# Loading the first filter block in two transfers, warming TensorE on a ready constant, and a new instruction order

## The chip, the cores and the metric

The kernel runs on one core of one Trainium2 chip. The metric is the device time of one execution in microseconds (us), the median of several. Before the change it is 344.8 us (three runs, 344.19 to 345.65).

The engines are named as in the profile: PE is TensorE (PEld its weight loads), DVE is VectorE, ACT is ScalarE, POOL is GpSimd, SP is SyncE, which issues most DMAs.

## What is computed

Two layers, each a long convolution block (A) and a gated feed-forward block (B), on 2048 positions of 512 channels in bf16. `q` is the stream x; the other inputs are k, v, a 4-tap filter, a 2048-tap filter per channel, a diagonal, and three weight matrices.

```python
def A(xn, k, v, shift_k, ssm_k, ssm_D):
    kv = causal_fir4(k, shift_k) * v
    y = causal_conv(kv, ssm_k)          # 2048 taps per channel, by FFT in the reference
    return xn * (y + kv * ssm_D)

def B(xn, w_gate, w_up, w_down):        # 512 -> 1792 -> 512
    return (silu(xn @ w_gate) * (xn @ w_up)) @ w_down

x = q
for layer in (0, 1):                    # same k, v and weights in both layers
    x = x + A(layernorm(x), k, v, shift_k, ssm_k, ssm_D)
    x = x + B(layernorm(x), w_gate, w_up, w_down)
```

## The kernel before, in words

**Tiling.** The 2048 positions are cut into four blocks c = 0 to 3 of 512; each block is 128 partitions of four consecutive rows (r = 0 to 3). A feed-forward unit is (layer, c, half): two of the four row sets, 256 columns on PE. There are 16 units, each with 224 matmuls of 256 columns (`pf`, gate and up, L311 through the helper `mm`) and 28 of 512 columns (`pd`, down, L990).

**The convolution** is done block by block with discrete Fourier transforms written as matmuls: `hn` (filter, channels on partitions) is transposed by PE into `pt`, copied to `hs`, transformed with the table `fwd` into `ps`, evacuated to `ev` and folded to `G`. The k block `kn` is transposed into `kTb` (L366, copies at L372 and L374), the 4-tap filter is 64 matmuls of `kTb` against diagonal tables `dg` (L311, `ps<-dg,kTb`), their result is multiplied by v (`vt`, L524, DVE), and `vt` is transformed (L458) into `X`. Products `X*G` give `Z`, `m`; inverse transforms (L797) give y for block 0. Then LayerNorm, product with y, the second LayerNorm, `z`, its transpose `zT`, and the first feed-forward matmul. The work up to there is called the opening here. The convolutions of the later blocks are threaded between the feed-forward matmuls.

**The opening's loads.** SP issues, in this order: `hn` of block 0 (L342, one transfer of 512 KB, 1 KB pieces), `kn` (L352), `vt`, `xc` (q), `hn` and `vt` of block 1, `wg_sb`, then DMA transposes and the other weights. Each is 512 KB but for the weights. ACT issues the two small ones, `tapR` and `drow` (L1067, L1069). DMAs share eight completion semaphores in turn, so the ninth waits for the first, and so on.

**Warming matmuls.** `warm` (L1264) issues matmuls that nobody reads, wherever the plan has PE idle in the first 32 us. Their operands are `wz`, a tile that DVE sets to 0.5 (L1050).

**LayerNorm statistics.** Most come from DVE (`ln_stats`, L809 to L812). Eight of them come from ACT (`ln_stats_act`): sums with accumulators (L828, L834), then `ve = sum/D + eps` on ACT (L838), then `rstd = ve^-0.5` on POOL (L840).

**The order.** Every operation is recorded with an engine, a cost and its reads and writes (`Plan.add`). The list `ORDER` ranks all 1568 operations; `Plan.order` sorts by it and gives each tile a slot of its ring, `Plan.issue` emits the sorted list. Each engine runs its instructions in that order. PSUM rings that matter in the opening: `pf` with four slots (transposes of `hn`, all `ps` of the first block, the `pf` tiles of the feed-forward), `pc` and `pd` with two each (transposes of `kn`, filter results).

What stands on PE at the start before: 22 warming matmuls, 4 small transposes of the taps (L1133), 5 warming, 16 transposes of `hn` (L477), 8 of `kn`, 8 transforms of `hs`, 8 transposes of `kn`, 6 transforms, 64 filter matmuls, 2 transforms, then the transforms of `vt`.

Of the kernel before, what the change touches and what calls it, by code (L numbers as in the profile page):

```python
# [9 lines left out]
P = 128  # L10
# [32 lines left out]
H_SPLIT = False  # L43
# [7 lines left out]
LASTV = True  # L51
ORDER = [
# [186 lines left out]
def kernel(  # L239
# [1024 lines left out]
    def warm(ring, slot, n):  # L1264
        t = psp.tile([P, P], F32, name="wm", tag=f"{ring}{slot}")
        for _ in range(n):
            nc.tensor.matmul(t[:], lhsT=wz.t[:], rhs=wz.t[:], start=True, stop=True)  # L1267
# [33 lines left out]
```

## Time and profile before

| what | value |
|---|---|
| median of three runs | 344.8 us |
| the profiled execution | 344.93 us |
| its span, first to last instruction | 343.2 us |
| PE busy | 336.4 us (98%), 2579 matmuls on record |
| DVE busy | 283.4 us (83%) |
| ACT busy | 253.9 us (74%) |
| POOL busy | 35.3 us (10%) |
| first feed-forward matmul starts | 33.58 us |
| last PE work ends | about 340.0 us |

The profiled execution is 1.73 us longer than its span; what lies outside the span is not seen. PE counts as busy while a matmul is in its pipe, so matmuls that follow each other closely overlap in the record; how far apart their starts are tells the rate, and the chain of waits, which sets such pieces end to end, shows it directly.

### The profile page before, as it was taken

Reading aid. Unit: us, or ns where it says so; the run is one execution under the profiler, and the core shown is the slowest. Engines: PE = TensorE matmul, PEld = TensorE weight load, DVE = VectorE, ACT = ScalarE, POOL = GpSimd, SP = SyncE. Lnnn points to the kernel's source line nnn. Section 1 sums busy time; section 2 is a strip of 40 time slices with the busy share of each in tenths; the row PEclk is TensorE's granted clock in tenths of the full one; section 3 lists DMA queues with packets and bytes.
Section 4 is the critical chain, followed back from the end, with each engine's and each line's share of the span. In section 5 each row is a group of like instructions: output and inputs, shape, how many; then the busy total and the mean of one; then the engine's idle time right before and its main releaser. Section 6 shows DMA issues by size and latency. Waiting matters only on the chain.

```text
span 343.2 us, 6553 instructions
## 1 busy us (share of the span) xinstructions
PE 336.4 (98%) x2579; PEld 248.6 (72%) x2610; DVE 283.4 (83%) x482; ACT 253.9 (74%) x504; POOL 35.3 (10%) x46
## 2 busy tenths in 40 slices
PE   8999999999999999999999999999999999999996
PEld 7756868768687676858586777768685877777783
DVE  8899999899999999899999999989998433726022
ACT  6999999899997765958789995779475464446261
POOL 4010100203111000103110100201101001000000
PEclk9999999999999999999999999999999999999999
DMA  7999218310116044040101014210101100110101
GB/s 273 336 316 341 52 27 112 77 32 0 34 31 94 14 95 138 2 94 3 32 2 46 2 46 79 76 32 1 32 0 33 35 13 0 39 39 8 24 26 37
DMA packets 42088, 22.95 MB, mean 67 GB/s; under 512 B 33861, under 2 KB 39882, under 8 KB 42058
## 3 DMA queue, kind: packets, MB, share of 16 engines
q1 hardware_dynamic: 41904, 22.47, 26.6%
q8 instruction: 20, 0.33, 0.4%
q14 instruction: 10, 0.08, 0.1%
q10 hardware_dynamic: 154, 0.07, 0.1%
HBM read 12.33 MB, written 2.10 MB: 42 GB/s over the span
## 4 chain that ended last, share of the span: by engine, by line
PE 91%; ACT 4%; DVE 3%; issue 1%
PE pf L311 54%; PE pd L990 28%; PE ps L311 6%; PE ps L458 1%; ACT H L419 1%; PE wm L1267 1%; DVE bnst L809 1%; ACT hs L487 1%; PE pt L477 1%; ACT X L419 0%; ACT n L859 0%; PE pt L366 0%; DVE m L540 0%; DVE t L665 0%; DVE Z L667 0%
## 5 line engine op out<-in xcount | busy, mean ns | idle before, releaser
L311 PE MATMUL pf<-zT,wu_sb 128*128 128x256 bf16 x896 | 110.4, 273 | 0.1
L311 PE MATMUL pf<-zT,wg_sb 128*128 128x256 bf16 x896 | 110.2, 273 | 0.2
L990 PE MATMUL pd<-wd_sb,ht 128*128 128x512 bf16 (+1 forms) x440 | 102.4, 372 | 1.2
L311 PEld LDWEIGHTS <-wu_sb 128*128 128x128 bf16 x896 | 87.7, 98 | 16.4
L311 PEld LDWEIGHTS <-wg_sb 128*128 128x128 bf16 x896 | 87.6, 98 | 16.5 <-issue 0.8
L974 ACT CAST ht<-pf 128x512 bf16<-128x512 f32 x112 | 64.0, 591 | 29.3 <-PE pf L311 29.1
L970 ACT ACTIVATE sg<-pf 128x512 bf16<-128x512 f32 x112 | 65.5, 603 | 17.4 <-PE pf L311 15.1
L990 PEld LDWEIGHTS <-ht 128*128 128x128 bf16 x462 | 45.2, 98 | 42.5
L977 DVE TENSOR_TENSOR ht<-ht,sg 128x1024 bf16<-128x1024 bf16 (+1 forms) x64 | 39.0, 617 | 24.0 <-ACT sg L970 18.7
L814 POOL TENSOR_TENSOR rstd<-ve,nhalf 128x2 f32<-128x2 f32 x24 | 23.0, 958 | 217.8 <-DVE ve L812 207.6
L1034 ACT CAST dn<-pd 128x512 bf16<-128x512 f32 x30 | 17.0, 589 | 21.0 <-PE pd L990 20.9
L809 DVE BATCH_NORM_STATS2 bnst<-xc 128x6 f32<-128x512 bf16 x48 | 31.6, 684 | 0.6
L419 ACT ACTIVATE X<-ps 128x512 bf16<-128x512 f32 x32 | 19.2, 611 | 4.0 <-PE ps L311 3.4
L653 DVE TENSOR_TENSOR t<-X,G 128x2048 bf16<-128x2048 bf16 x18 | 21.9, 1218 | 0.1
L657 DVE TENSOR_TENSOR t<-X,G 128x2048 bf16<-128x2048 bf16 x18 | 21.9, 1216 | 0.0
L1037 DVE TENSOR_TENSOR xc<-xc,dn 128x1024 bf16<-128x1024 bf16 x15 | 10.3, 689 | 13.4 <-ACT dn L1034 13.2
L665 DVE TENSOR_TENSOR t<-t,t 128x2048 bf16<-128x2048 bf16 x12 | 14.7, 1222 | 0.3
L667 DVE TENSOR_TENSOR Z<-Z,t 128x2048 bf16<-128x2048 bf16 x12 | 14.6, 1220 | 0.2
L840 POOL TENSOR_TENSOR rstd<-ve,nhalf 128x2 f32<-128x2 f32 x8 | 8.7, 1088 | 59.2 <-ACT ve L838 59.1
L419 ACT ACTIVATE H<-ps 128x512 bf16<-128x512 f32 x24 | 13.8, 610 | 0.1
L886 DVE TENSOR_TENSOR n<-n,Yk 128x1024 bf16<-128x1024 bf16 x15 | 10.3, 688 | 4.1 <-ACT n L859 3.8
L604 ACT ACTIVATE kc<-kTb,tapF 128x512 bf16<-128x512 bf16 x16 | 12.1, 783 | 0.0
(105 smaller groups left out, 323.3 us busy)
## 6 DMA issues: line engine op xcount, KB each, us to landing
hn<-in_A_ssm_k_dram SPq DMA_DIRECT2D x4, 512.0 KB, 4.1
vt<-in_A_v_dram SPq DMA_DIRECT2D x4, 512.0 KB, 5.9
xc<-in_A_q_dram SPq DMA_DIRECT2D x4, 512.0 KB, 5.3
out_dram<-xc SPq DMA_DIRECT2D x15, 128.0 KB, 1.8
wg_sb<-in_B_w_gate_dram SPq DMA_DIRECT2D x1, 1792.0 KB
wu_sb<-in_B_w_up_dram SPq DMA_DIRECT2D x1, 1792.0 KB, 8.5
wd_sb<-in_B_w_down_dram SPq DMA_DIRECT2D x1, 1280.0 KB, 12.0
kn<-in_A_k_dram SPq DMA_DIRECT2D x1, 512.0 KB, 4.5
```

Of the source, the lines that this page charges most:

```text
L311: nc.tensor.matmul(o, lhsT=lhsT, rhs=rhs, start=(n == 0), stop=(n == len(terms) - 1))
L419: add("ACT", act(D), lambda: nc.scalar.activation(out=view(), in_=ps.t[:], func=ACT.Copy, scale=scale), r=[ps], w=[(buf, keys)], conv=conv)
L653: dve(n * D, lambda t1=t1, part=part: nc.vector.tensor_mul(out=t1.t[:], in0=x.t[:, sl, 0, :], in1=g.t[:, sl, part, :]), [(x, key(slots, (0 ...
L657: dve(n * D, lambda t2=t2, part=part: nc.vector.tensor_mul(out=t2.t[:], in0=x.t[:, sl, 1, :], in1=g.t[:, sl, 1 - part, :]), [(x, key(slots ...
L665: dve(n * D, lambda t1=t1, t2=t2, comb=comb: nc.vector.tensor_tensor(out=t1.t[:], in0=t1.t[:], in1=t2.t[:], op=comb), [t2], [t1], conv=conv)
L809: add("DVE", 0.6, lambda st=st, i=i: nc.vector.bn_stats(out=st.t[:], in_=xs[c].t[:, i, :]), r=[(xs[c], (i,))], w=[st])
L814: add("POOL", pw, lambda: nc.gpsimd.tensor_tensor(out=rstd.t[:], in0=ve.t[:], in1=nhalf.t[:].to_broadcast((P, n)), op=ALU.pow), r=[ve, nha ...
L970: add("ACT", act(D), lambda ps=ps, o=o, sg=sg: nc.scalar.activation(out=sg.t[:, o:o + 2, :], in_=ps.t[:], func=ACT.Silu), r=[ps], w=[(sg, ...
L974: add("ACT", act(D), lambda ps=ps, o=o, ht=ht: nc.scalar.copy(out=ht.t[:, o:o + 2, :], in_=ps.t[:]), r=[ps], w=[(ht, (o // 2,))], due=(uni ...
L977: dve(n * W, lambda sg=sg, ht=ht: nc.vector.tensor_mul(out=ht.t[:], in0=ht.t[:], in1=sg.t[:]), [sg], [ht], due=(unit, k / pairs, 0.0, "h"))
L990: nc.tensor.matmul((pds[o] if not cs.start else pds[HP]).t[:, cs], lhsT=ht.t[:, q, o * P:(o + 1) * P], rhs=wt["d"].t[:, ft, cs], start=(ft ...
L1034: add("ACT", act(D), lambda o=o: nc.scalar.copy(out=dn.t[:, o, :], in_=pds[o].t[:]), r=[pds[o]], w=[(dn, (o,))], due=(unit, 1.0, 3.0, "h"))
```

## The change

Five edits, one of them large.

1. `H_SPLIT = True`: block 0 of `hn` is loaded in two transfers of 256 KB (channel tiles 0 and 1, then 2 and 3), and each row set is transposed in two parts, one for each transfer.
2. `warm` uses a bf16 tile of ones that the framework fills before the kernel begins; `wz` and its memset on DVE go. The count of warming matmuls may reckon from 0.0 in place of 0.3.
3. `VE_D = True`: the eight `ve` of `ln_stats_act` are made by DVE (one `tensor_scalar` of 128x2) in place of ACT.
4. `ORDER` is a new list, of 1572 operations, for all engines and the whole kernel.
5. Line numbers move by one to five.

```diff
-H_SPLIT = False
+H_SPLIT = True
...
+VE_D = True
 ORDER = [
...
-                            n = int((start - max(t, 0.3) - 0.3) / 0.106)
+                            n = int((start - max(t, 0.0) - 0.3) / 0.106)
...
-        add("ACT", TINY, lambda: nc.scalar.activation(out=ve.t[:], in_=sm.t[:, n:2 * n], func=ACT.Identity, scale=1.0 / D, bias=eps.t[:]),
-            r=[(sm, range(n, 2 * n)), eps], w=[ve])
+        if VE_D:
+            add("DVE", 0.08, lambda: nc.vector.tensor_scalar(out=ve.t[:], in0=sm.t[:, n:2 * n], scalar1=1.0 / D, scalar2=LN_EPS,
+                                                             op0=ALU.mult, op1=ALU.add), r=[(sm, range(n, 2 * n))], w=[ve])
...
-    wz = whole("wz", [P, P])
-    add("DVE", 0.07, lambda: nc.vector.memset(wz.t[:], 0.5), w=[wz], due=-80)
+    ones = nc.const_aps.tensor(1.0, (P, P), BF16)
...
-            nc.tensor.matmul(t[:], lhsT=wz.t[:], rhs=wz.t[:], start=True, stop=True)
+            nc.tensor.matmul(t[:], lhsT=ones, rhs=ones, start=True, stop=True)
```

What the new order makes of the opening, engine by engine:

- SP: `hn` first half, `kn`, `hn` second half, `vt`, `xc`, and on as before. So `kn` stands between the halves. Later, both parts of `wd_sb` go ahead of `xc` of block 1, and `kTb` of block 2 ahead of `hn` of block 2.
- PE: 25 warming matmuls, the 4 tap transposes, 8 transposes of the first half of `hn`, 8 of the second, 1 warming, 12 transposes of `kn`, 2 transforms of `hs`, 4 transposes of `kn`, 8 transforms, 4 filter matmuls, 4 transforms, 60 filter matmuls, 2 transforms, then `vt`. In the first feed-forward unit the up tiles run ahead of the gate tiles.
- POOL: the identity is made before `fq`, the counting table that the angles `ph` need.
- DVE and ACT: the same operations up to the first `zT`, but for `wz` and `ve`, in a slightly different order; before the first `zT` ACT evacuates the same tiles. In the first feed-forward unit ACT has by its first `nmr` four tiles of `pf` evacuated, where it had five.
- All engines: from the first feed-forward matmul on PE has the same matmuls in another interleaving.

More of the change, by code (lines that the diff above doesn't have):

```diff
@@ L837, in ln_stats_act @@
         ve, rstd = new("ve", "ve", [P, n], F32), new("rs", "rstd", [P, n], F32)
-        add("ACT", TINY, lambda: nc.scalar.activation(out=ve.t[:], in_=sm.t[:, n:2 * n], func=ACT.Identity, scale=1.0 / D, bias=eps.t[:]),
-            r=[(sm, range(n, 2 * n)), eps], w=[ve])
+        if VE_D:
+            add("DVE", 0.08, lambda: nc.vector.tensor_scalar(out=ve.t[:], in0=sm.t[:, n:2 * n], scalar1=1.0 / D, scalar2=LN_EPS,
+                                                             op0=ALU.mult, op1=ALU.add), r=[(sm, range(n, 2 * n))], w=[ve])
+        else:
+            add("ACT", TINY, lambda: nc.scalar.activation(out=ve.t[:], in_=sm.t[:, n:2 * n], func=ACT.Identity, scale=1.0 / D, bias=eps.t[:]),
+                r=[(sm, range(n, 2 * n)), eps], w=[ve])
         add("POOL", PWA, lambda: nc.gpsimd.tensor_tensor(out=rstd.t[:], in0=ve.t[:], in1=nhalf.t[:].to_broadcast((P, n)),
```

116 rows, old and new, of the table ORDER are left out of this document.

## Prediction, made blind

> **What bounds the kernel now.** I read the stages first: busy time of each engine in stretches of the span (columns: stretch, length, then PE, PEld, DVE, ACT, POOL, granted clock, DMA share, GB/s).
>
> ```profile
> 0.00:14.00 14.00, 12.85 (x137) 10.80 (x139) 11.62 (x35) 10.57 (x23) 3.64 (x14) 1.00 0.87 321
> 20.00:33.50 13.50, 12.65 (x117) 8.06 (x118) 13.14 (x31) 13.50 (x28) 0.69 (x1) 1.00 1.10 355
> 33.50:50.00 16.50, 16.40 (x135) 12.99 (x135) 16.33 (x25) 16.37 (x36) 1.65 (x2) 1.00 0.24 35
> 50.00:150.00 100.00, 99.48 (x731) 72.11 (x739) 96.86 (x155) 83.25 (x168) 10.66 (x10) 1.00 0.31 60
> 150.00:340.00 190.00, 189.12 (x1432) 141.49 (x1446) 139.65 (x231) 124.85 (x241) 17.62 (x18) 1.00 0.12 28
> ```
>
> From 33.5 to 340 PE never rests. That is not the pipe's overlap alone. In the chain of waits, 48 `pf` matmuls take 5.24 us (0.1092 each) and 16 `pd` take 3.45 us (0.216 each). The program's matmuls after the first `pf`, each at such a price (0.0558 for 128 columns), make 305.9 us. The first `pf` starts at 33.58, and 33.58 + 305.9 = 339.5 is where the last PE work is (it ends at 340.0). So there are no holes to win after 33.58; an order can only make holes there. The tail, 340.0 to 343.2, is last evacuation and store, alike in both programs. **All gain must come from the opening.**
>
> So next the opening: the chain of waits in order of time (start, length, what).
>
> ```profile
> 1.04 2.53 PE wm L1267 x22
> 3.57 0.22 PE pt L1133 x4
> 3.79 0.66 PE wm L1267 x5
> 4.49 1.86 PE pt L477 x16
> 6.35 0.85 PE pt L366 x8
> 7.21 0.75 PE ps L311 x3
> 8.01 1.03 PE ps L311 x4
> 9.03 0.45 PE pt L366 x8
> 9.48 5.08 PE ps L311 x71
> 14.62 4.49 PE ps L458 x20
> ```
>
> PE is the chain from 4.49 to 19. Two things are to be seen. First, it began real work when `hn` landed: issued at 0.72, 3.6 us to landing, 4.3. Second, PE's rate doubles on the way: eight transposes of `kn` take 0.85 at 6.35 and 0.45 at 9.03, so 0.106 each and then 0.056. The page's clock row shows full clock throughout; the spacing doesn't. In the record of single starts it changes between 7.0 and 7.4.
>
> **Part 1, two transfers (the largest term).** The landings decide:
>
> ```profile
> 0.72 0.45 SPq L342 DMA_DIRECT2D hn<-in_A_ssm_k_dram  x1
> 1.24 0.48 SPq L352 DMA_DIRECT2D kn<-in_A_k_dram  x1
> kn<-in_A_k_dram SPq DMA_DIRECT2D x1, 512.0 KB, 4.5
> ```
>
> `kn` landed at 1.24 + 4.5 = 5.74, when 1 MB had come. In the new order the first half of `hn` goes first, then `kn`, then the second half: the same 1 MB, with the second half now last. If one queue serves in order of issue, it lands at about **5.7**, where the whole of `hn` landed at 4.3; `kn` lands some 0.6 earlier (256 KB at 390 GB/s). The first half: by the half-microsecond rates (223, 352, 383, 406 GB/s from 2.0) 256 KB are across by 2.9, the whole by 3.7, and landing was 0.6 behind that, so 3.5. The rest of the loads issue one slot (0.5) later; the DMA share is about 1 from 2.5 to 15, so bytes set their times and this costs nothing; without that cover it would be 0.5.
>
> PE then goes so: warming from 0.82 (DVE's first instruction starts there, released by the same barrier; PE's start at 1.04 waited for `wz`), 25 x 0.1067 to 3.5, taps to 3.75, first half 8 x 0.107 to 4.6. Then it waits for the second half until 5.9 (PE started 0.19 behind the landing at 4.3), and is through at 6.75. Before, the transposes were through at 6.15 + 0.05, so **0.6 late**. Behind them: 1 warming and 12 of `kn`, at 0.107 until 7.28 and 0.056 after, to 7.73. By then `hs` is there: ACT's copy of 0.59 from 6.35, DVE's of 0.42 from 6.55. The other two end at 7.4 and 7.85 (an ACT `dg` of 0.40 stands between). From 7.73: 2 transforms (0.43), 4 of `kn` (0.22), 8 transforms (1.73), 4 filter (0.22), 4 transforms (0.86), 60 filter (3.35): 14.54. Before, the filter ended at 14.19. PE has no earlier slot to give: **+0.35**. DVE's last product with v starts behind that and ends at 15.43, where it ended at 15.08 (12.39 + 2.69), so the delay passes on to `X`, `Z` and the first `z`.
>
> POOL makes `fq` after the identity, so the angles start some 0.4 later and `fwd` is ready near 5.7; PE uses it at 7.7. Hidden by the wait above; if that were gone it would be the next thing late, but 0.4 early still.
>
> **Part 2, warming.** PE starts 0.22 earlier; real work still waits for a landing: 0 by itself. The memset of `wz` (0.17) had DVE's idle start around it: 0. What it may do to the rate is a rival below.
>
> **Part 3, `ve`.** ACT loses 8 x 0.296 = 2.4 us, DVE gains 8 x 0.169 = 1.35 (the rate of its own `ve`, L812). Most of it lies beside PE's full stretch and is worth 0 there. In the opening there is one: ACT's at 17.90, behind which ACT sat idle 0.27 for PE, so 0 is won; DVE's on a chain that is busy to 30.55, so up to +0.17. Against it, DVE waited 0.23 at 30.77 for ACT's `ks` (L514), which now comes earlier. Together between -0.25 and +0.2, taken as **-0.05**, by those two rows.
>
> **Part 4, the rest of the order.** Same operations before the first `zT`. In the first unit ACT is full (16.37 of 16.50), and PE takes a new `pf` slot as soon as ACT empties one. ACT now has four tiles out at `nmr`, not five. Carrying its rows on (0.59 a tile, 0.81 `n`, 0.30 `nmr`, 0.55 `X`), the slot for the ninth tile is free at 41.3 and PE wants it at 41.0: a hole of 0.3, none if ACT runs as closely as before. Nearest row below: no hole in 306 us. I take **+0.1**, ends 0 and 0.4. Later holes: 0, end 1. `hn` of block 2 issues behind `kTb` (35.4, it was 24.3), lands within 8 us by the slowest such row; its first reader is at 46.6.
>
> **Sum** on the profiled execution: 344.93 + 0.35 - 0.05 + 0.1 = **345.3**. That execution is 0.13 above the median of the runs shown, so I make no correction.
>
> **Rival 1, the rate doubles later (slower than before).** In the trace the doubling came 6.3 us after the first warming matmul, over two gaps of about 0.2 and 0.3, and 2.8 after the last gap. The new order puts a gap of 1.3 at 4.6 to 5.9. If a gap starts the count again, the doubling comes between 5.9 + 2.8 = 8.7 and 5.9 + 6.3 = 12.2; take 10.4. Each microsecond of half rate past 7.3 costs half of one while PE is the chain: (10.4 - 7.3)/2 = 1.55, so 346.85, from 346.0 to 347.8. It is slower than 346.5 from a doubling at 9.7. Against it: a gap of 0.3 at 4.2 was borne. [...]
>
> **Rival 2, faster.** Either the rate doubles before 5.9, because PE started earlier, or the second half lands with the first, by 4.7. The former takes 8 x 0.05 off the second transposes and 5 x 0.05 off `kn`: 345.3 - 0.65 = 344.65. The latter leaves no wait: transposes done by 5.6, 0.6 before the old ones, 344.2. Take 344.4. For it: the runs before spread from 344.19 to 345.65, so something in the opening moves by that much.
>
> **Rival 3, the order makes holes later,** at DVE's full stretch (96.86 of 100 from 50 to 150): 1 to 2 us, 346.8. Against it: PE waits for nothing there now.
>
> **Chances.** Forecast 0.45 (345.0 to 345.8), rival 1 0.25, rival 2 0.25, rival 3 0.05. Half a per cent, 1.7 us, is about what a measurement can tell here, so faster means under 343.1 and slower over 346.5. Faster 0.04 (rival 2 with everything early), slower 0.17 of rival 1 and 0.03 of rival 3: 0.20. Same 0.76. Range: 344.2 (rival 2) to 347.0 (rival 1's middle).
>
> **What would show it.** The second half of `hn` landing near 5.7 and PE idle from 4.6; the rate's change near 7.3; the last filter matmul near 14.5; the first `pf` near 33.9; no hole over 0.3 after it. I am wrong if the halves land together, if the rate changes before 5 or past 9, or if the first `pf` starts before 33.5.

## The result, and the profile after

The changed kernel takes **348.19 us** (median of 13 executions, 345.46 to 350.25) where the kernel before takes 345.0 beside it (344.08 to 346.83): a ratio of 1.009, interval 1.0062 to 1.0118. It is slower, and outside the predicted range of 344.2 to 347.0. Its executions lie in three groups, near 345.5, 348 and 349.7; the spread of 4.8 us, against 2.75 before, is itself a finding.

The profiled execution is one of 347.47, with a span of 345.6 (before 343.2). The stages come first, as before: stretch, length, busy time of PE, PEld, DVE, ACT and POOL, clock, DMA share, GB/s.

```profile
0.00:14.00 14.00, 10.99 (x98) 8.74 (x100) 9.32 (x31) 8.69 (x18) 3.73 (x13) 1.00 0.86 305
50.00:150.00 100.00, 99.49 (x731) 72.23 (x740) 97.73 (x156) 82.59 (x162) 11.56 (x10) 1.00 0.23 51
150.00:340.00 190.00, 189.05 (x1425) 141.00 (x1442) 140.73 (x238) 126.84 (x245) 17.62 (x19) 1.00 0.15 33
```

From 50 on PE is as full as it was; the first 14 us are where it lost, 98 matmuls in place of 137. The chain of waits there (start, length, what), and behind it the timeline of PE's transposes (the bracket is the idle time just before, and what ended it):

```profile
1.74 5.25 DMA hn<-in_A_ssm_k_dram
7.04 1.04 PE pt L478 x8
8.08 0.11 PE wm L1271
8.19 1.28 PE pt L367 x12
9.47 0.62 PE ps L312 x2
10.09 0.22 PE pt L367 x4
10.80 5.68 PE ps L312 x73
16.91 3.45 PE ps L459 x16
```

```profile
4.44 1.04 PE L478 MATMUL pt<-ident,hn 128*128 128x128 bf16 x8 [0.64 <-DMA hn<-in_A_ssm_k_dram]
7.04 1.04 PE L478 MATMUL pt<-ident,hn 128*128 128x128 bf16 x8 [1.56 <-DMA hn<-in_A_ssm_k_dram]
```

Three things differ from the forecast. (A correction that no number hangs on: the transfer issued first holds channel tiles 2 and 3, not 0 and 1 as the section on the change has it.) The second half of `hn` lands at 6.99, not 5.7, and the first at 4.39, not 3.5. `kn`'s 12 transposes take 1.28, 0.107 each, long past 7.28; in the record of single starts the rate doubles at 9.72, and the trace's clock records have an event at the same moment (9.724). The clock column reads 1.00 all the same. The last filter matmul then starts 2.1 later than before, and the first `pf` at 35.83 where it was 33.58.

One step further back lie the bytes. The busy time of the engines from 2.0 to 5.7, before and after, with the DMA queues' GB/s in the last column:

```profile
2.00:5.70 3.70, 3.65 (x36) 3.27 (x35) 3.52 (x15) 2.69 (x6) 1.51 (x3) 1.00 1.02 340
2.00:5.70 3.70, 2.84 (x27) 2.29 (x25) 3.25 (x15) 2.62 (x5) 1.15 (x3) 1.00 0.93 272
```

So the loads came at 272 GB/s where they came at 340: the second half was late because its bytes were, and `kn` (5.65) came only 0.06 earlier than before.

Behind the first `pf` the view of waits has one left (waited for: us in total, times, longest):

```profile
PE pf L312 <- ACT ht L979: 0.3, 1, 0.3
```

It is the hole for the ninth tile's slot, at 42.9; by the starts of the matmuls it is 0.44. So 2.25 in the opening and 0.44 there make 2.69. The last matmul starts 2.63 later than before, and the span grows by 2.4, since what follows that matmul is 0.23 shorter.

**Two theories.** A, mine: the time went to the two landings and to the rate that doubles late, and the gap in PE's work is what makes it late. B: the new order, or `ve` on DVE, costs it. Within A it was open whether the late transfer or the late rate weighs more, and why each is late.

### The profile page after: what moved, and what is told of

Same layout as the page of the kernel before. It is cut to its first block, busy times and chain, and to the rows that moved or that the text cites. A ratio compares the mean times of both kernels' runs of the same rounds, so it can differ in the third digit from the quotient of the medians.

```text
span 345.6 us, 6551 instructions
## 1 busy us (share of the span) xinstructions
PE 337.1 (98%) x2578; PEld 248.8 (72%) x2611; DVE 283.2 (82%) x489; ACT 252.3 (73%) x496; POOL 37.5 (11%) x46
## 4 chain that ended last, share of the span: by engine, by line
PE 91%; DVE 3%; ACT 2%; DMA 2%; issue 1%; POOL 1%; SPq 0%
PE pf L312 55%; PE pd L995 28%; PE ps L312 6%; PE ps L459 2%; DMA hn<-in_A_ssm_k_dram 2%; ACT H L420 1%; ACT n L864 1%; DVE m L541 1%; PE pt L478 1%; POOL rstd L845 0%; PE pt L367 0%; DVE H L547 0%; DVE H L558 0%; DVE bnst L810 0%; ACT nmr L857 0%
## 5 line engine op out<-in xcount | busy, mean ns | idle before, releaser
L995 PE MATMUL pd<-wd_sb,ht 128*128 128x512 bf16 (+1 forms) x440 | 100.6, 372 | 1.1
L815 POOL TENSOR_TENSOR rstd<-ve,nhalf 128x2 f32<-128x2 f32 x24 | 24.9, 1036 | 215.0 <-DVE ve L813 165.8
L845 POOL TENSOR_TENSOR rstd<-ve,nhalf 128x2 f32<-128x2 f32 x8 | 8.9, 1112 | 61.0 <-DVE ve L840 61.0
L668 DVE TENSOR_TENSOR Z<-Z,t 128x2048 bf16<-128x2048 bf16 x12 | 14.6, 1219 | 0.1
L605 ACT ACTIVATE ka<-kTb,tapF 128x512 bf16<-128x512 bf16 x16 | 12.2, 788 | 0.0
```

Source lines behind the costliest of these rows:

```text
L815: add("POOL", pw, lambda: nc.gpsimd.tensor_tensor(out=rstd.t[:], in0=ve.t[:], in1=nhalf.t[:].to_broadcast((P, n)), op=ALU.pow), r=[ve, nha ...
L995: nc.tensor.matmul((pds[o] if not cs.start else pds[HP]).t[:, cs], lhsT=ht.t[:, q, o * P:(o + 1) * P], rhs=wt["d"].t[:, ft, cs], start=(ft ...
```

## The experiments

Each ratio is to the kernel before on the same chip, its interval in brackets. Nothing of the reference's computation is left out in any of them; extra warming matmuls produce nothing that is read.

**The change without the split.** One transfer of `hn`, all the rest as changed (order, ones, `ve` on DVE); the five ranks of the operations that the split adds are dropped.

```diff
-H_SPLIT = True
+H_SPLIT = False
...
+ORDER = [x for n, x in enumerate(ORDER) if n not in (9, 32, 35, 38, 41)]
```

> The changed kernel with hn of block 0 in one transfer and each row set turned in one part; all other ranks, the ones and VectorE's ve are kept. The planner puts five warming matmuls between the taps and hn, so PE is without a gap from 0.8 to 7. Theory (split and gap cost everything): 344 to 345, first feed-forward matmul at 33.5 or before. Rival (the rest of the new order costs): 347 or more. If the hole of 0.3 at the ninth pf tile is all that the rest costs, 0.3 over the best runs of before.

Measured: 344.58, ratio 1.0002 (0.9993 to 1.0012). B falls: the whole loss needs the split. In its profile the first `pf` is at 33.16, 0.4 earlier than in the first profile of before, and two holes (0.43 at 40.2, 0.33 at 92) give that back.

**Filling the gap.** The change, with 16 more warming matmuls between the two halves' transposes.

```diff
             o.emit()
+            if o.n == 35:
+                warm("pc", 1, 16)
```

> The changed kernel with sixteen more warming matmuls between PE's work on the first and on the second half of hn, so that PE does not idle while it waits; loads unchanged, the second half lands near 6 to 7 as before the edit. Theory (the gap delays the doubling): the rate doubles before 7.7, and the time falls by 1.5 to 2.5 us to about 346. Rival (the late landing alone costs): no change, 348. Rival (rest of the order): no change.

Measured: 345.53 (344.9 to 346.07), ratio 1.0026 (1.0016 to 1.0037). The three groups are gone. By the ratios, 0.64 of the 0.9 per cent came from the gap's effect on the rate (about 2.2 us) and 0.26 (0.9 us) from the rest, if the data came as late in the other executions as in the profiled one (second half 6.67). The chain:

```profile
1.73 4.94 DMA hn<-in_A_ssm_k_dram
6.72 0.64 PE pt L480 x8
7.41 0.67 PE pt L369 x12
```

The spacing is 0.056 from 4.7 on, so the added matmuls were through early and PE still waited 0.97. Only 0.16 us of them lie ahead of the doubling; the evidence here is that all eleven executions lie below 346.1, not this one profile.

**Both halves ahead of `kn`.** The change, with the second half of `hn` issued right behind the first.

```diff
+ORDER[9] = 1.5
```

> The changed kernel with the second half of hn issued right behind the first, kn after both; the planner then also puts nine warming matmuls, not one, behind the transposes. Theory (the second half lands late, and PE's wait for it delays the doubling of the rate): the second half lands near 4.4, PE's wait before it is under 0.3 us, the rate doubles by about 7.6, and the time falls from 348.2 to 344.5 to 345.5. Rival (the rest of the new order costs it): stays at 347 or more. Rival (only the landing costs, not the rate): 346 to 347, with the doubling still past 9.

Measured: 347.62, ratio 1.0059 (1.0033 to 1.0084). My expectation failed. The halves landed at 3.48 and 5.00, early enough, but `kn`, now third, landed at 8.16, and PE stood still as before, one operation later:

```profile
5.04 0.64 PE L479 MATMUL pt<-ident,hn 128*128 128x128 bf16 x8 [0.34 <-DMA hn<-in_A_ssm_k_dram]
5.52 0.69 PE L1272 MATMUL wm<-const-bfloat16-1.0 128*128 128x128 bf16 x9
8.20 1.46 PE L368 MATMUL pt<-ident,kn 128*128 128x128 bf16 x12 [2.00 <-DMA kn<-in_A_k_dram]
```

Eight transposes in 0.64, then twelve in 1.46: a doubled rate was taken away again. The clock records of this run have three events, full at 4.493, half at 7.906, full at 11.320, each 3.413 behind the one before.

**The split on the kernel before.** Its order and its `wz`, with the halves of `hn` around `kn` and the five added operations at fitting ranks.

```diff
-H_SPLIT = False
+H_SPLIT = True
...
+LATE = {10: 31.5, 31: 38.1, 33: 38.2, 35: 38.3, 37: 38.4}
+ORDER = [y for n, x in enumerate(ORDER) for y in ([LATE[n], x] if n in LATE else [x])]
```

> The kernel before with one part of the change alone: hn of block 0 in two transfers with kn between them and the transposes in two parts of eight; the order otherwise that of before, warming on wz. Theory: PE waits about 1.3 us or more between the parts, the rate doubles past 8.5 in most runs, and the time rises from 345.0 to 347 to 348.5, which is all of the change's loss. Rival (the rest of the new order costs): 345 to 345.7.

Measured: 347.11, ratio 1.007 (1.005 to 1.0089): the split alone brings most or all of the loss (the two intervals overlap). Second half at 7.38, rate doubled at 12.04.

```profile
7.43 1.04 PE L479 MATMUL pt<-ident,hn 128*128 128x128 bf16 x8 [2.66 <-DMA hn<-in_A_ssm_k_dram]
8.26 0.31 PE L1269 MATMUL wm<-wz 128*128 128x128 bf16 x1
```

**The late rate alone.** The kernel before without the warming matmuls of the opening; its loads are untouched.

```diff
-                            n = int((start - max(t, 0.3) - 0.3) / 0.106)
+                            n = int((start - max(t, 0.3) - 0.3) / 0.106) if t > 20 else 0
```

> The kernel before with the warming matmuls of the opening taken out: the loads stay as they are (hn whole, landing near 4.3, kn near 5.7), and only the moment at which TensorE's rate doubles can move. Theory (the time of the changed kernel was lost to half rate that lasts longer): PE is nearly idle until 4.5, so the first stretch of 3.41 us with little idle time ends between 7.9 and 11.3; 0.6 to 4.0 us more of half rate than before (7.28), half of it lost: 344.8 to 346.5, with the last filter matmul at 14.5 to 16.1 and the first pf between 33.9 and 35.6. Rival (what costs is the wait for the late transfer, and the rate matters little because the opening waits for ScalarE and VectorE anyway): within 0.3 us of before, last filter matmul near 14.2.

Measured: 346.22, ratio 1.0042 (1.0025 to 1.0059), inside the theory's 344.8 to 346.5. `hn` landed at 4.21 and `kn` at 5.47, no later than before; the rate doubled at 9.64, and the first `pf` came at 34.65. That is 1.07 later than in the first profile of before, for 2.36 us more of half rate. The halved rate shows in the chain:

```profile
4.26 1.89 PE pt L477 x16
6.15 0.85 PE pt L366 x8
7.01 3.09 PE ps L311 x8
10.10 0.45 PE pt L366 x8
```

Eight transforms of 512 columns take 3.09, though the rate doubles within them; at the full rate they take 1.73.

**The halves on two queues.** The change, with the second half issued by ACT.

```diff
+ORDER[9] = 0.5
...
+                e, q = ("SP", nc.sync) if n else ("ACT", nc.scalar)
-                o = add(eng, 0.5, lambda sl=sl: q.dma_start(
+                o = add(e, 0.5, lambda sl=sl, q=q: q.dma_start(
```

> The changed kernel with the second half of hn issued by ScalarE, first on its queue at about 0.7, beside the first half on SP's queue; kn is then the second transfer of SP's queue. The planner puts 30 warming matmuls ahead of hn's 16 transposes in a row. Theory A (a third transfer behind two others on one queue is what comes late): both halves land by 4.6 and kn by 5.9, the rate doubles before 6, and the time is 343.8 to 344.8. Theory B (any split leaves some of the 16 rings behind, whatever the queue): one of the halves, or kn, has one or two of its 16 pieces over 0.4 us behind the others, at 6.4 or later, PE waits there, and the time is 345.3 to 347.5. Rival to both (the taps, now behind the second half on ScalarE's queue, land over 0.5 us later and hold PE): PE's wait ahead of the taps grows from 0.1 to over 0.5.

Measured: 344.23, ratio 1.0000 (0.9986 to 1.0015). The loss is gone. The halves landed at 4.08 and 4.41, `kn` at 5.67; PE waited only for the taps, 0.26:

```profile
4.37 0.29 PE L1139 MATMUL pt<-ident,tapR 4*128 4x4 bf16 x4 [0.26 <-DMA tapR<-in_A_shift_k_dram]
4.60 1.08 PE L480 MATMUL pt<-ident,hn 128*128 128x128 bf16 x16
5.52 0.39 PE L1273 MATMUL wm<-const-bfloat16-1.0 128*128 128x128 bf16 x4
```

The rate doubled at 4.14. The outcome is theory A's, but its reason isn't proved by it. The transfer that is third on SP's queue (now `vt`) still came with the last of its 16 pieces at 8.32 where 15 were in by 7.10; nobody waits for it there. In this run the split left neither of its own parts behind: its theory B falls.

**Warming right through, on the kernel before.** 36 warming matmuls on ones, from 0.76 to 5.0, in place of 27.

```diff
-                            n = int((start - max(t, 0.3) - 0.3) / 0.106)
+                            n = int((start - max(t, 0.0) - 0.3) / 0.106) + (3 if t < 20 else 0)
...
-            nc.tensor.matmul(t[:], lhsT=wz.t[:], rhs=wz.t[:], start=True, stop=True)
+            nc.tensor.matmul(t[:], lhsT=ones, rhs=ones, start=True, stop=True)
```

> The kernel before with its one load of hn and its order, but with 36 warming matmuls on the ready constant, from 0.76 until hn lands near 4.4, where it had 27 on a tile of its own from 1.04 with 0.6 us of holes. Theory: the stretch that ends between 3.9 and 4.9 has under 0.75 us of idle time, so the rate doubles there, some 2.7 us earlier than before (7.28); hn's 16 transposes take 0.9 instead of 1.7, then PE waits some 0.2 for kn (5.7); of the 1.35 us that the half rate costs in 4.5 to 7.28 about 0.9 is left: 343.6 (343.2 to 344.0), first pf near 32.7, no later hole since the order is the old one. Rival (the opening is then bound by kn, the evictions and the arrival of vt): 344.2 to 344.6, as in the run with one load and the new order, whose rate doubled at 5.96 and whose time did not move.

Measured: 345.26, ratio 1.0022 (1.001 to 1.0034). Both expectations missed the time. The opening did what the theory said: rate doubled at 4.74, first `pf` at 32.83 (0.75 earlier). Then PE waits, by its starts 0.9 at 90.6, where it never waited, and 0.37 at 132, where the first profile of before has 0.21:

```profile
PE pf L311 <- DMA zT<-z: 1.0, 2, 0.7
91.73 0.49 PE L311 MATMUL pf<-zT,wu_sb 128*128 128x256 bf16 x3 [0.74 <-DMA zT<-z]
```

With the 0.75 these make up the 0.3 by which the profiled execution is longer than that of before. Who held `zT` shows one step further back. DVE makes `z`, and SP issues the transposing transfers of it (here first, then before):

```profile
85.59 0.73 DVE L864 TENSOR_SCALAR z<-xc,mv,rstd 128x512 bf16<-128x512 bf16 x2
86.39 1.98 SPq L893 DMA_TRANSPOSE zT<-z  x1
86.34 0.73 DVE L864 TENSOR_SCALAR z<-xc,mv,rstd 128x512 bf16<-128x512 bf16 x2
87.14 1.19 SPq L893 DMA_TRANSPOSE zT<-z  x1
```

`z` and the first issue were 0.75 earlier, as PE was, so DVE did not hold them, although it is busy 96.86 of 100 us in this stretch in the kernel before. That one issue took 1.98 in place of 1.19, and so the second of the pair was through at 89.68 against 89.64. What the opening won was lost there. A 16 KB transfer on the DMA queue q8, named "instruction", began within the long issue, at 86.7; before, the nearest on q8 began at 91.8. In the thirteen traces 46 transposing transfers issued behind 30 us (not counting those of `kTb`) took over 1.6 us to issue, and all began at most 0.5 behind the start of such a transfer or had one begin in them. That this transfer is the cause was not tested; in the runs with two queues such an issue of over 2 us at 86 made PE wait for nothing.

**The hole at 40 mended.** To the run with two queues, and to the run with one transfer (with 36 warming matmuls in place of 30), one edit: ACT's two `nmr` and the first `n` of that tile pair stand behind the eviction that PE waits for.

```diff
+ORDER[235], ORDER[237], ORDER[234] = 268.2, 268.4, 268.6
```

> The kernel with the second half of hn on ScalarE's queue, and beside it ScalarE's tiny shift and its two normalising steps at 38.6 to 39.9, which wait for POOL's rstd, put behind the eviction of a filled pf tile for which PE waits (hole of 0.45 at 39.9 in that run). If that hole is all that the order gives away, the hole is under 0.1 and the time is 343.8 (343.4 to 344.1), faster than before. Rival (the time is given back later: ScalarE's normalising comes 0.5 later, or a transfer that was hidden is waited for, as zT at 90.6 in the run with the long warming): a new hole of 0.3 or more after 40, and 344.1 to 344.6.

> The changed kernel with hn in one transfer, 36 warming matmuls in place of 30, and the same mend at 40. If two queues bring nothing beside the warming, the rate doubles by 4.9, the first pf is at 32.9 or earlier, and the time is within 0.3 of the run with two queues and the mend; if the halves on two queues bring something of themselves (hn complete at 4.4 and not 4.55), it is 0.2 to 0.5 longer.

Measured: with two queues 343.84, ratio 0.9981 (0.9968 to 0.9995); with one transfer 343.96, ratio 0.9983 (0.9971 to 0.9994). The hole at 40 is gone in both, none has taken its place, and both are faster than before, and so than the change, by a small but measurable 0.2 per cent. Their medians differ by 0.12: that the two queues bring anything that one transfer doesn't can't be seen. In the profiled executions the rate doubled at 3.38 (two queues) and at 6.65 (one transfer; the expected "by 4.9" failed there, and with it the first `pf` by 32.9: it came at 33.74).

**Both kernels once more, unaltered.**

> The changed kernel, unaltered: a second profile. If the moment at which TensorE's rate doubles sets the time of an execution, and that moment falls differently in each execution (its runs lie near 345.5, 348 and 349.8), then this execution's time stands to the first one's (347.47, doubled at 9.72) as 0.5 us per us of its own moment, give or take 0.5 for the landing of the second half. Rival: the moment is the same and the time differs, or the other way round.

> The kernel before, unaltered: a second profile. Expected: first transfers as in the first profile (hn whole at 4.3 to 4.6, kn by 5.9, single late pieces of the third transfer, vt, which nobody waits for before 14); its rate doubles at another moment than 7.28, and its time differs from 344.93 by half of that difference (0 to 1.2 us shorter, as its runs lie between 343.7 and 345.7). Rival: the rate doubles at 7.28 again.

Measured: the changed kernel at 345.13, doubled at 5.01, second half landed at 6.03, first `pf` at 33.61. The kernel before at 344.70, doubled at 6.60, first `pf` at 33.28: 0.23 shorter, where half of the earlier doubling would be 0.34, and without the late pieces of `vt` that I had expected. The chain of the former, to hold against the one above:

```profile
1.74 4.29 DMA hn<-in_A_ssm_k_dram
6.08 0.64 PE pt L478 x8
6.77 0.67 PE pt L367 x12
8.58 5.68 PE ps L312 x73
```

The same program, 2.34 us apart, and 2.22 of that in the first `pf`. It adds up: the landing differs by 6.99 - 6.03 = 0.96, and the first execution worked at half rate from 7.04 to 9.72, which costs 2.68/2 = 1.34. The expected 0.5 us for each us of the moment hit the number, 345.1, but partly by luck, because the landing moved too and a part of the late stretch was spent waiting.

## Why the rate doubles when it does

All profiled executions together (times in us; "needed" is the last landing that PE waits for in the opening):

| kernel | needed landing | rate doubles | first `pf` | profiled time |
|---|---|---|---|---|
| before | 4.30 `hn` | 7.28 | 33.58 | 344.93 |
| before, again | 4.47 `hn` | 6.60 | 33.28 | 344.70 |
| before, no warming | 4.21 `hn` | 9.64 | 34.65 | 345.79 |
| before, warmed through | 4.38 `hn` | 4.74 | 32.83 | 345.25 |
| before, split | 7.38 second half | 12.04 | 37.05 | 347.94 |
| after | 6.99 second half | 9.72 | 35.83 | 347.47 |
| after, again | 6.03 second half | 5.01 | 33.61 | 345.13 |
| after, gap filled | 6.67 second half | 4.7 | 34.27 | 345.58 |
| after, `kn` last | 8.16 `kn` | 4.49, lost, 11.32 | 36.73 | 348.07 |
| after, one transfer | 4.55 `hn` | 5.96 | 33.16 | 344.73 |
| after, two queues | 4.41 second half | 4.14 | 32.83 | 344.01 |
| after, two queues, mended | 4.67 taps | 3.38 | 33.10 | 343.83 |
| after, one transfer, mended | 4.16 `hn` | 6.65 | 33.74 | 344.53 |

In the run with `kn` last three events of the clock lie 3.413 apart. The other records agree with that step: in each of the twelve profiles that have them the full rate, once it stays, lasts 337.919 or 334.506 us, which is 99 or 98 times 3.4133. I read this as a clock that is set in windows of that length; the records show the step, not what sets it.

Going back from each doubling in such steps, I add up the time in which PE had no matmul, from its starts and spacings (the four small transposes of the taps counted as idle). By this count every window at whose end the rate doubled held at most 0.79 us without one (0.73 in the first profile of after, 0.78 in the second, 0.79 with two queues and the mend, 0.70 or less in the others). The windows just ahead of them held 0.93 or more (0.93 in before, 2.1 in after). The window that took the rate away held 2.4; windows with 1.2 to 1.3 kept it (after, again, 5.01 to 8.42; two queues, mended, 3.38 to 6.80). The line near 0.8 to 0.9 belongs to this way of counting: with the transposes of the taps as work, the 0.93 of before is 0.75, and no such line is left. How much idle time a window may hold is thus not shown. And where the windows begin differs from execution to execution of one program: the doublings of the two profiles of before are 0.68 apart (7.28 and 6.60), those of after 4.71 (9.72 and 5.01), neither a whole number of steps.

On this reading, with the old loads PE is busy almost without a break from about 1 us (0.6 without a matmul from 1.04 to 7.28 in the first profile of before), and if 0.79 is borne, a window that counts ends by an estimated 7.5, whatever the phase. With the split, the gap (1.3 to 1.6 us in the two profiles of after, 2.7 in the split of before) spoils the window in which it lies: in the second profile of after, where the rate had doubled at 5.01, nothing was lost; in the first, and in the split of before, it doubled only at 9.72 and 12.04. That fits the changed kernel's groups near 345.5 and 348, and with the gap filled all eleven executions lie between 344.90 and 346.07. The third group, near 349.7, has five of the thirteen executions and none of the profiles: at half a microsecond of time for each microsecond of the moment it would take a doubling near 14, or a still later landing, or a rate that is lost again. Which it is stays open.

The two profiled executions of after differ by 0.7 per cent (347.47 and 345.13), which is most of this change's loss.

## Why the prediction was wrong

- **All gain or loss comes from the opening:** right. 2.25 of the span's 2.4 lie ahead of the first `pf`.
- **Part 1, the landing:** "the same 1 MB, with the second half now last ... lands at about 5.7" is the first step that failed. It was 6.99 and, the second time, 6.03, and the first half varied from 3.52 to 4.39. In the profiled execution PE resumed at 7.04 in place of 5.9: **1.14 us**. The sum took the pace of the bytes from the old loads. It was 272 GB/s from 2.0 to 5.7, 297 the second time, against 340 and 368 in the two profiles of before. In all five profiles with the halves on SP's queue it was 272 to 297, in the other eight 316 to 368. So `kn` did not come 0.6 earlier either.
- **Part 1, the rate:** doubling at 7.28 "as before" is the second. It was 9.72. Half rate lay over PE's work for 2.68 us (7.04 to 9.72), where I had 1.38 (5.9 to 7.28): **0.65 us**. By medians this term is the greater: filling the gap took back 0.64 of 0.9 per cent. I treated the moment as a property of the program; it belongs to the execution (9.72 and 5.01 in two of the same program). The kernel before had given a hint, its spread of 1.5 us over three runs, which I used only for rival 2.
- Together 1.79 of the 2.17 between forecast and profiled time; of the remaining 0.38 the hole gives 0.34 (0.44 for 0.1).
- **Part 2, warming, 0 by itself:** not shown alone. With one transfer and the rest of the change the ratio is 1.0002, but in that profile the rate doubled at 5.96, the opening was 0.42 shorter, and two holes gave it back. Where PE was warmed without a gap, in the kernel before, the rate doubled at 4.74 and the first `pf` came 0.75 earlier.
- **Parts 3 and 4, -0.05 and +0.1:** right in sum by the same run, but partly by luck: the hole for the ninth tile came where it was worked out, with 0.44 for 0.3. That it was at stake at all showed only when it was closed, where the opening was early. A second hole in that run, 0.33 at 92, was forecast as 0 and was offset by the shorter opening. In the changed kernel it did not come, so **rival 3** is not what happened.
- **Rival 1** is what happened, as to place and sign: a doubling between 8.7 and 12.2, found at 9.72 (and 11.32 and 12.04 in the two split variants). Its price of 1.55 lacked the later landing, so 346.85 was still too low. That "a gap starts the count again" is not the mechanism: behind the end of the gap the doubling came after 2.7 (after), 3.1 (`kn` last) and 4.6 us (split of before), no fixed count, and in the second profile of after the gap of 1.3 behind 5.01 cost no clock. A moment left free would have served better: with the doublings that the runs showed, 3.38 to 12.04, its price spreads from 0 to over 2 us ((12.04 - 7.28)/2 = 2.38).
- **Rival 2** happened too, in the second profile: the rate early, but the landing at 6.03 ate the gain.

## What to carry to other kernels

Before you split a transfer to start earlier, ask what the engine does between the parts: a start that is 0.05 to 0.8 us earlier and a gap of 1.3 us or more cost more here than waiting for the whole with warming matmuls. The moment of the clock that I read in one profile was a draw, not a constant (9.72, then 5.01); give such a moment a spread, here the 3.413 of one step or more, and look at the spread of the kernel's runs for it. A gain in the opening is not yet a gain in the time: 0.75 us were lost again at one transfer whose issue took 0.79 longer. And when a wait moves, follow it back to its first late step before you name the fullest engine as its cause; DVE, busy 97 of 100 us, had kept up.

## What the runs showed of the hardware beyond that

In twelve of the thirteen profiled executions single 4 KB pieces of SP's loads that began between 4.7 and 6.2 us of the span took 0.4 to 1.4 us, where most take 0.159 (the run warmed through has one of them; the second profile of before has only one of 0.39, and its transfers all ended close together). In six of them some began earlier, from 2.5 on, and in the first profile of after 1 KB pieces of the first half, of which most take 0.046, took up to 1.03 between 2.4 and 3.6; that half landed at 4.39. A ring (one of the 16 parts in which a transfer arrives) that met a slow piece stayed behind: in the first profile of before `vt` had twelve pieces in by 7.2 and the other four at 7.8, in the run with `kn` last every later transfer ended 1.3 behind its neighbours. With the old order the transfer in flight at that time is `vt`, which PE needs at 14.6; the split put a needed transfer there. What holds those pieces up, and why the halves on SP's queue came at the lower pace, stays open. The transposing transfer of `inv` is not the cause of all: with two queues SP issued it at 6.06 and slow pieces began at 4.98, in the split of before at 6.01 and 3.6.
